# Three edits to an attention, expert and swish kernel: y's sums as a pipeline, a branch with four idle products, a split table moved by one step

## The chip, the cores and the metric

The kernel runs on one core of a Trainium2 chip. The metric is the device time of one execution in microseconds (us), the median over runs; lower is better. An engine has its own instruction queue and works through it in order: PE (TensorE, matrix products), ACT (ScalarE), DVE (VectorE), POOL (GpSimd) and SP (SyncE, which issues most of the DMAs). Engines wait for each other and for DMAs on semaphores.

## The reference, cut to what matters

Attention without softmax over four batches, a top-1 mixture of experts with a fixed number of slots, and a swish layer:

```python
attn = np.maximum(z @ z.T / S, 0) ** 2            # per batch, S = 3072, z is S x 64
x = (u * (attn @ v)).reshape(B * S, 256)
e = argmax(x @ w_gate)                            # 8 experts, 384 slots each
slot[e] <- the first 384 tokens that chose e      # the others give zero rows
y = relu(slot @ w1[e]) @ w2[e] * gate             # 256 -> 1024 -> 256
h = y @ w_in; out = (h * sigmoid(h)) @ w_out      # 256 -> 2048 -> 256
```

All products are fp32: an operand is kept as a high part (rounded to fp32r) and a low part (what is left), and a product is the sum of three products of parts. "To split" a tile is a cast for the high part and a subtraction for the low part.

## The kernel before

**Attention.** The tokens come in chunks: six of 512 (batch 0), then one of 384 (chunk 6, the first of batch 1). A step (`attend`) handles one block of 128 keys: `scores` (two products into a PSUM bank `ps_s`), relu and square on ACT and DVE, `square` (ACT casts `ah`, DVE subtracts `al`) and, three steps after the scores, `values` (six products into `ps_a`). A chunk has KT = 24 steps, so chunk 6 starts at step TL = 144. PE's order within a step is scores, then values.

**The table around the steps.** `at(t, f)` notes work for the end of step t; each engine then gets it in the order in which it was noted. For batch 1, v and z have to be loaded and split again in six groups g of four key blocks: `load_z`, `load_v` (SP), and four steps later `split_z` (POOL) and `split_v` (cast on ACT, subtraction on POOL). The tiles `zr` of `load_z` and `zq` of a chunk's own queries (`Chunk.load`, split by POOL into `qt`) share two buffers; `rawt` for v has two buffers as well (g % 2). A load whose buffer is not yet free makes SP wait, and all loads behind it. POOL also sums up converted weights (`Convert`, L215, L218, L220) and scatters finished token rows (L463).

**The branch.** Expert 0 is computed ahead of the branch (`inward(0, ...)`): its second half `expert_out(d)` ends with a copy of y on ACT (L634) and a store to `yT` by SP (L635), for d = 0 and 1. Then `unless_full` (L949) branches on all engines if a slot is still free; here it never is. Behind the branch stand the transposes of unit 1 (`transposes`, L598) and its hidden products (`hidden`).

**The swish layer.** y is read back by blocks of 1024 slots (`Slots.load`), and seven block products stand in for eight (`quad`): they need sums of y's four blocks, each split in two parts. `Slots.steps` is a generator: b11 and b21 as they are, t1 = b12 - b11, t2 = b22 - t1, t3 = b22 - b12, t4 = b21 - t2, and b22. Before, every `put` casts on ACT (L724) and subtracts on DVE (L725) and every difference (L733, L738, L743, L748) stands in a step of its own, in the order in which the values depend on each other. For the first slots the steps run beside the last unit's `expert_out(0)`, two at a time (`prepare`), and the rest in the first `quad`; later slots take one step for each `side()` of a quad. A `quad` begins with two blocks on b11 and b21, copies the first (`p1`, L1093) on ACT, and goes on with blocks on t2 and t1 into the same bank.

Of the kernel before, what the change touches and what calls it, by code (L numbers as in the profile page):

```python
# [8 lines left out]
F32 = mybir.dt.float32  # L9
# [11 lines left out]
P = 128  # L21


def raw(ap):
    return ap.bitcast(F32)
# [3 lines left out]
def attention_moe_swish_kernel(  # L29
# [13 lines left out]
    nc = tc.nc  # L43
    w_in, w_out = w_in.bitcast(I32), w_out.bitcast(I32)
    B, S, D = v.shape
    E, _, F = w1.shape
    F2 = w_out.shape[0]
    KT = S // P
    GK = 4
    NG = KT // GK  # L50
    NH = D // P
    LAG = 3
    SQ = 4
    QC = 512
    QB = 384
    NTM = QC // P
    FT, FT2 = F // P, F2 // P
    SLOT = -(-cap // P) * P
    NSLOT = E * SLOT
    QM = min(QB, SLOT)  # L60
# [10 lines left out]
    wts = ctx.enter_context(tc.tile_pool(name="wts", bufs=1))  # L71
    dram = ctx.enter_context(tc.tile_pool(name="dram", bufs=1, space=DRAM))
    disp = dram.tile([NSLOT, ROW], F32, name="disp")
    yT = dram.tile([NH, P, NSLOT], F32, name="yT")
# [12 lines left out]
    def bank(kind):  # L87
        return pools["ps_" + kind].tile([P, 512], F32, tag=kind, name="ps_" + kind)
# [63 lines left out]
    wih = wts.tile([P, NH, F2], F32R, name="wih")  # L152
    wil = wts.tile([P, NH, F2], F32R, name="wil")
    wo = wts.tile([P, FT2, 2 * D], F32R, name="wo")

    def head(eng, hi, x):

# [90 lines left out]
    class Stream:  # L248
# [5 lines left out]
        def at(self, t, f):  # L254
            self.todo.setdefault(t, []).append(f)
# [318 lines left out]
    class Unit:  # L574
# [45 lines left out]
        def expert_out(self, d, fs=range(FT)):  # L620

            Q, x = self.Q, self.x
            t = bank("s")
            ds = slice(d * P, (d + 1) * P)
            for n, f in enumerate(fs):
                q, r = divmod(f, FT // 2)
                wh, wl = x.w2h[q][:, r, ds], x.w2l[q][:, r, ds]
                mm(t[:, :Q], lhsT=wh, rhs=hh[f][:, :Q], start=(n == 0), stop=False)
                mm(t[:, :Q], lhsT=wl, rhs=hh[f][:, :Q], start=False, stop=False)
                mm(t[:, :Q], lhsT=wh, rhs=hl[f][:, :Q], start=False, stop=(n == FT - 1))  # L630
                if n % 2:
                    yield
            y = pools["el"].tile([P, QC], F32, tag="r", name="y", bufs=3)
            nc.scalar.copy(y[:, :Q], t[:, :Q])  # L634
            nc.sync.dma_start(out=yT[d][:, self.off:self.off + Q], in_=y[:, :Q])  # L635

# [64 lines left out]
    class Slots:  # L703
# [12 lines left out]
                self.b[d, h] = t  # L716

        def steps(self):
            V = nc.vector
            parts = list(self.parts)  # L720

            def put(n, x):
                hi, lo = self.t[n] = parts.pop(0), parts.pop(0)
                nc.scalar.copy(hi, x)  # L724
                V.tensor_sub(lo, x, raw(hi))  # L725

            b = self.b
            put("b11", b[0, 0])
            yield
            put("b21", b[1, 0])  # L730
            yield
            t1 = self.temps()
            V.tensor_sub(t1, b[0, 1], b[0, 0])  # L733
            yield
            put("t1", t1)
            yield
            t2 = self.temps()
            V.tensor_sub(t2, b[1, 1], t1)  # L738
            yield
            put("t2", t2)  # L740
            yield
            t3 = self.temps()
            V.tensor_sub(t3, b[1, 1], b[0, 1])  # L743
            yield
            put("t3", t3)
            yield
            t4 = self.temps()
            V.tensor_sub(t4, b[1, 0], t2)  # L748
            yield
            put("t4", t4)  # L750
            yield
            put("b22", b[1, 1])
            yield

        def product(self, f, g, j, last):
# [34 lines left out]
    TL = nb0 * KT  # L790
# [11 lines left out]
    def idle(n):  # L802

        nc.tensor.matmul(wps[:, :n], lhsT=warm[:, :P], rhs=warm[:, :n], start=True, stop=True)
# [26 lines left out]
            at(c * KT - (11 if c < nb0 else 8), chunks[c].load)  # L831
            at(c * KT - 6, lambda c=c: chunks[c].split(nc.gpsimd))
    for g in range(NG):

        t = TL - KT + (g + 1) * GK + LAG + 1
        at(t - 4, lambda g=g: (b1.load_z(g), b1.load_v(g)))
        at(t, lambda g=g: (b1.split_z(g, nc.gpsimd, nc.gpsimd), b1.split_v(g, eng=nc.scalar)))

    free = [t for t in range(CV_A, TL + CV_B) if (t < KT or CV_OFF <= (t - LAG + 1) % KT < KT - 1)]
# [84 lines left out]
    if early:  # L924
        inward(0, first, False)
    st.finish()


    def unless_full(label=None):
# [53 lines left out]
    for h in range(NH):  # L983
        u.transposes(h)
        drain()
        u.split_x(h)

    blocks = Blocks()

# [19 lines left out]
    for i in range(first, len(units)):  # L1009
        if i + 1 < len(units):  # L1010

            inward(i, lambda f: next(work, None) if f > 4 and f != FT else None)
        else:
            for _ in work:
                pass
            stage += halves([pools["ut"].tile([P, 1024], F32, tag="ut", name="stage0"),
                             pools["xr"].tile([P, NTM * ROW], F32, tag="xr", name="stage1")])
            slots[0].load()
            n = [0]

            def prepare(f):
                n[0] += 1
                if n[0] == FT:

                    raws = [wts.tile([P, GK * D], F32R, tag=f"rawt{k}", name=f"part{k}") for k in range(4)]
                    sets[0] = halves(raws) + halves(big[0:3])
                    slots[0].parts = sets[0]
                    prepare.it = slots[0].steps()
                if n[0] > FT:
                    for _ in range(2):  # L1030
                        next(prepare.it, None)

            inward(i, prepare)


            second = units[i].expert_out(1, [2, 3, 0, 1] + list(range(4, FT)))
# [201 lines left out]
```

## Time and profile before

| what | value |
|---|---|
| runs before | median 737.92 us of 3 (736.95 to 738.42) |
| the profiled execution's own time | 734.02 us |
| its span | 732.2 us |
| PE busy | 714.6 us (98%) |
| DVE, ACT, POOL busy | 521.4 (71%), 502.8 (69%), 265.9 us (36%) |
| waits of PE that end by another engine | ACT L358: 4.9 us in 2; SP L949: 2.0 us |

Stretches below are in us from the start of the span. In a timeline row the brackets at the end hold the idle time of the engine just before the instruction and what ended it. `x6` stands for six instructions that follow each other. PEclk is the clock that TensorE was granted, as a share of 2.4 GHz; 0.50 is 1.2 GHz. A PE row's length runs to a modelled end; the next product can start before it.

### The profile page before, as it was taken

Reading aid. Unit: us, or ns where it says so; the run is one execution under the profiler, and the core shown is the slowest. Engines: PE = TensorE matmul, PEld = TensorE weight load, DVE = VectorE, ACT = ScalarE, POOL = GpSimd, SP = SyncE. Lnnn points to the kernel's source line nnn. Section 1 sums busy time; section 2 is a strip of 40 time slices with the busy share of each in tenths; the row PEclk is TensorE's granted clock in tenths of the full one; section 3 lists DMA queues with packets and bytes.
Section 4 is the critical chain, followed back from the end, with each engine's and each line's share of the span. In section 5 each row is a group of like instructions: output and inputs, shape, how many; then the busy total and the mean of one; then the engine's idle time right before and its main releaser. Section 6 shows DMA issues by size and latency. Waiting matters only on the chain.

```text
span 732.2 us, 11355 instructions
## 1 busy us (share of the span) xinstructions
PE 714.6 (98%) x3951; PEld 637.7 (87%) x3951; DVE 521.4 (71%) x955; ACT 502.8 (69%) x986; POOL 265.9 (36%) x246
## 2 busy tenths in 40 slices
PE   8999999999999998998999999899999999999996
PEld 6888888888888877998999999799999999999896
DVE  6787877878778765862677777668767876666790
ACT  6777778777787867864666666566557665665671
POOL 7771505314253289254577676000004000040004
PEclk9999999999999999999999999999999999999999
DMA  5833515134155323452555554020101000010001
GB/s 182 288 140 122 181 49 190 51 123 138 41 203 174 116 74 97 133 166 88 206 178 176 178 177 149 12 69 15 44 1 51 9 1 0 1 58 1 1 1 58
DMA packets 50668, 72.18 MB, mean 99 GB/s; under 512 B 3446, under 2 KB 38684, under 8 KB 50608
## 3 DMA queue, kind: packets, MB, share of 16 engines
q1 hardware_dynamic: 48160, 65.03, 27.2%
q0 software_dynamic: 2448, 6.39, 2.4%
q8 instruction: 32, 0.52, 0.3%
q14 instruction: 28, 0.23, 0.1%
HBM read 46.05 MB, written 25.77 MB: 98 GB/s over the span
## 4 chain that ended last, share of the span: by engine, by line
PE 50%; issue 1%; ACT 0%; DVE 0%; POOL 0%; POOLq 0%; DVEq 0%; ACTq 0%
PE ps_s L766 18%; PE ps_a L240 8%; PE ps_s L240 7%; PE ps_a L1050 5%; PE ps_a L1051 5%; PE ps_a L1052 5%; PE ps_a L598 1%; POOL out L777 0%; ACT part L724 0%; POOLq L1234 0%; DVE part L725 0%; DVE temp L743 0%; DVE temp L738 0%; DVE temp L733 0%; ACT u L1093 0%
## 5 line engine op out<-in xcount | busy, mean ns | idle before, releaser
L240 PE MATMUL ps_a<-ah,big 128*128 128x512 f32 (+1 forms) x672 | 184.0, 390 | 4.9 <-ACT ah L358 4.9
L240 PEld LDWEIGHTS ps_a<-ah,big 128*128 128x128 f32 x672 | 124.5, 189 | 26.4 <-ACT ah L358 4.9
L359 DVE TENSOR_TENSOR al<-ps_s,ah 128x512 fp32r<-128x512 f32 (+1 forms) x168 | 111.4, 663 | 29.3 <-ACT ah L358 29.3
L345 ACT ACTIVATE r<-ps_s 128x512 f32<-128x512 f32 (+1 forms) x168 | 98.3, 585 | 44.7 <-PE ps_s L240 39.6
L350 DVE TENSOR_TENSOR ps_s<-ps_s,r 128x512 f32<-128x512 f32 (+1 forms) x132 | 89.2, 676 | 42.8 <-ACT r L345 41.2
L777 POOL DMA_INDIRECT out<-rows,ids x24 | 25.4, 1060 | 244.2 <-ACT rows L774 238.4
L766 PEld LDWEIGHTS ps_s<-wo,big 128*128 128x128 f32 x792 | 103.2, 190 | 5.0
L566 POOL TENSOR_TENSOR big<-rawt,big 128x512 fp32r<-128x512 f32 x64 | 90.3, 1437 | 43.5 <-ACT big L161 42.9
L240 PE MATMUL ps_s<-qt,kz 128*128 128x512 f32 (+1 forms) x336 | 105.6, 391 | 0.0
L766 PE MATMUL ps_s<-wo,big 128*128 128x256 f32 x792 | 105.2, 282 | 0.0
L240 PE MATMUL ps_a<-al,big 128*128 128x512 f32 (+1 forms) x336 | 101.6, 383 | 0.0
L358 ACT CAST ah<-ps_s 128x512 fp32r<-128x512 f32 (+1 forms) x168 | 95.7, 569 | 3.5 <-DVE ps_s L350 3.3
L240 PEld LDWEIGHTS ps_s<-qt,kz 128*128 128x128 f32 x336 | 63.4, 190 | 11.5 <-POOL kz L295 0.4
L240 PEld LDWEIGHTS ps_a<-al,big 128*128 128x128 f32 x336 | 63.1, 189 | 11.6
L463 POOL DMA_INDIRECT disp<-xr,idx x27 | 28.4, 1052 | 107.9 <-ACT ps_s L348 79.8
L240 PE MATMUL ps_a<-qt,big 128*128 128x384 f32 x336 | 61.2, 341 | 0.2 <-ACT qt L604 0.2
L240 PEld LDWEIGHTS ps_a<-qt,big 128*128 128x128 f32 x336 | 59.7, 192 | 0.8 <-ACT qt L604 0.5
L161 ACT CAST big<-rawt 128x512 fp32r<-128x512 f32 x86 | 51.5, 624 | 6.4 <-DMA rawt<-in_v 6.4
L1063 DVE TENSOR_TENSOR sg<-ps_a,sg 128x512 f32<-128x512 f32 x72 | 47.9, 684 | 2.2
L1073 DVE TENSOR_TENSOR big<-sg,big 128x512 fp32r<-128x512 f32 x66 | 45.1, 686 | 6.2 <-ACT big L1072 5.0
L766 PEld LDWEIGHTS ps_s<-wo,late_c 128*128 128x128 f32 x348 | 45.9, 189 | 2.6
L1072 ACT CAST big<-sg 128x512 fp32r<-128x512 f32 x66 | 41.0, 622 | 9.2 <-DVE sg L1063 8.8
(227 smaller groups left out, 1245.5 us busy)
## 6 DMA issues: line engine op xcount, KB each, us to landing
rawt<-in_w SPq DMA_DIRECT2D x32, 512.0 KB, 5.0
out<-zero SPq DMA_DIRECT2D x16, 768.0 KB, 7.3
rawt<-in_v SPq DMA_DIRECT2D x11, 512.0 KB, 4.1
rawt<-in_w_in SPq DMA_DIRECT2D x8, 512.0 KB, 5.1
disp<-empty SPq DMA_DIRECT2D x6, 528.0 KB, 7.1
xg<-disp SPq DMA_DIRECT2D x8, 396.0 KB, 3.3
zr<-in_zT SPq DMA_DIRECT2D x12, 256.0 KB, 4.1
ut<-in_uT SPq DMA_DIRECT2D x6, 512.0 KB, 4.4
```

What stands on the lines that cost most here:

```text
L161: eng.copy(hi, x)
L240: nc.tensor.matmul(*a, **k)
L345: nc.scalar.activation(r[:, :Q], s[:, :Q], AF.Relu)
L350: nc.vector.tensor_mul(s[:, :Q], s[:, :Q], r[:, :Q])
L358: nc.scalar.copy(ah[:, :Q], a[:, :Q])
L359: nc.vector.tensor_sub(al[:, :Q], a[:, :Q], raw(ah[:, :Q]))
L566: nc.gpsimd.tensor_sub(ls[q][:, cs], rawt[r0 + q][:, cs], raw(hs[q][:, cs])))
L766: nc.tensor.matmul(o, lhsT=w[:, cs], rhs=wo[:, f, c:c + D], start=m not in self.seen, stop=last and n == 2, skip_group_check=True)
L1050: nc.tensor.matmul(ps, lhsT=ah, rhs=th, start=start, stop=False, skip_group_check=True)
L1063: nc.vector.tensor_mul(sg, src, sg)
L1072: nc.scalar.copy(gh, g)
L1073: nc.vector.tensor_sub(gl, g, raw(gh))
```

## The change

Three places are edited.

1. `Slots.steps` is written as a pipeline: the low part of a value stands beside the next difference and the next cast. It now has 9 steps, not 11, and `prepare` takes 2, 1, 1, 2 of them at its four calls, not 2 each; with that the cast of t3 and the difference t4 are still the last work ahead of the first quad.
2. The store of expert 0's second y tile (d = 1) is no longer issued ahead of the branch: y stays in a tile of its own (`y0`), and SP gets the store behind the branch's transposes in the program. Four idle products of 512 columns (bf16, `warm`) are put on PE ahead of the branch.
3. The table of batch 1: every load and split of z and v comes one step earlier, but for the split of group 1, which stays where it was.

```diff
--- before.py
+++ after.py
@@ -152,6 +152,8 @@
     wih = wts.tile([P, NH, F2], F32R, name="wih")
     wil = wts.tile([P, NH, F2], F32R, name="wil")
     wo = wts.tile([P, FT2, 2 * D], F32R, name="wo")
+    y0 = wts.tile([P, QM], F32, name="y0")
+    later = []
 
     def head(eng, hi, x):
 
@@ -630,9 +632,14 @@
                 mm(t[:, :Q], lhsT=wh, rhs=hl[f][:, :Q], start=False, stop=(n == FT - 1))
                 if n % 2:
                     yield
-            y = pools["el"].tile([P, QC], F32, tag="r", name="y", bufs=3)
+            keep = self.first and d == NH - 1
+            y = y0 if keep else pools["el"].tile([P, QC], F32, tag="r", name="y", bufs=3)
             nc.scalar.copy(y[:, :Q], t[:, :Q])
-            nc.sync.dma_start(out=yT[d][:, self.off:self.off + Q], in_=y[:, :Q])
+            store = lambda: nc.sync.dma_start(out=yT[d][:, self.off:self.off + Q], in_=y[:, :Q])
+            if keep:
+                later.append(store)
+            else:
+                store()
 
 
 
@@ -716,40 +723,49 @@
                 self.b[d, h] = t
 
         def steps(self):
+
             V = nc.vector
             parts = list(self.parts)
-
-            def put(n, x):
-                hi, lo = self.t[n] = parts.pop(0), parts.pop(0)
-                nc.scalar.copy(hi, x)
-                V.tensor_sub(lo, x, raw(hi))
-
             b = self.b
-            put("b11", b[0, 0])
-            yield
-            put("b21", b[1, 0])
-            yield
-            t1 = self.temps()
-            V.tensor_sub(t1, b[0, 1], b[0, 0])
-            yield
-            put("t1", t1)
-            yield
-            t2 = self.temps()
-            V.tensor_sub(t2, b[1, 1], t1)
-            yield
-            put("t2", t2)
-            yield
-            t3 = self.temps()
-            V.tensor_sub(t3, b[1, 1], b[0, 1])
-            yield
-            put("t3", t3)
-            yield
-            t4 = self.temps()
-            V.tensor_sub(t4, b[1, 0], t2)
-            yield
-            put("t4", t4)
-            yield
-            put("b22", b[1, 1])
+
+            def hi(n, x):
+                self.t[n] = parts.pop(0), parts.pop(0)
+                nc.scalar.copy(self.t[n][0], x)
+
+            def lo(n, x):
+                V.tensor_sub(self.t[n][1], x, raw(self.t[n][0]))
+
+            def diff(x, y):
+                t = self.temps()
+                V.tensor_sub(t, x, y)
+                return t
+
+            hi("b11", b[0, 0])
+            yield
+            lo("b11", b[0, 0])
+            hi("b21", b[1, 0])
+            yield
+            lo("b21", b[1, 0])
+            t1 = diff(b[0, 1], b[0, 0])
+            yield
+            t2 = diff(b[1, 1], t1)
+            hi("t1", t1)
+            yield
+            lo("t1", t1)
+            t3 = diff(b[1, 1], b[0, 1])
+            hi("t2", t2)
+            yield
+            lo("t2", t2)
+            t4 = diff(b[1, 0], t2)
+            hi("t3", t3)
+            yield
+            lo("t3", t3)
+            hi("t4", t4)
+            yield
+            lo("t4", t4)
+            hi("b22", b[1, 1])
+            yield
+            lo("b22", b[1, 1])
             yield
 
         def product(self, f, g, j, last):
@@ -831,9 +847,9 @@
             at(c * KT - (11 if c < nb0 else 8), chunks[c].load)
             at(c * KT - 6, lambda c=c: chunks[c].split(nc.gpsimd))
     for g in range(NG):
-
-        t = TL - KT + (g + 1) * GK + LAG + 1
+        t = TL - KT + (g + 1) * GK + LAG
         at(t - 4, lambda g=g: (b1.load_z(g), b1.load_v(g)))
+        t += g == 1
         at(t, lambda g=g: (b1.split_z(g, nc.gpsimd, nc.gpsimd), b1.split_v(g, eng=nc.scalar)))
 
     free = [t for t in range(CV_A, TL + CV_B) if (t < KT or CV_OFF <= (t - LAG + 1) % KT < KT - 1)]
@@ -924,6 +940,9 @@
     if early:
         inward(0, first, False)
     st.finish()
+    wps = bank("a")
+    for _ in range(4):
+        idle(QC)
 
 
     def unless_full(label=None):
@@ -984,6 +1003,8 @@
         u.transposes(h)
         drain()
         u.split_x(h)
+    for store in later:
+        store()
 
     blocks = Blocks()
 
@@ -1027,7 +1048,7 @@
                     slots[0].parts = sets[0]
                     prepare.it = slots[0].steps()
                 if n[0] > FT:
-                    for _ in range(2):
+                    for _ in range(2 if n[0] in (FT + 1, FT + 4) else 1):
                         next(prepare.it, None)
 
             inward(i, prepare)
```

**DVE, where the sums of the first slots begin** (`part` and `big` are the parts, `stage` the blocks of y, `temp` the differences). Before:

```order
L725 TENSOR_TENSOR part_7299<-stage_7213,part_7299 128x512
L725 TENSOR_TENSOR part_7300<-stage_7213,part_7300 128x512
L733 TENSOR_TENSOR temp<-stage_7214,stage_7213 128x512
L725 TENSOR_TENSOR part_7301<-temp,part_7301 128x512
L738 TENSOR_TENSOR temp<-stage_7214,temp 128x512
L725 TENSOR_TENSOR part_7302<-temp,part_7302 128x512
L743 TENSOR_TENSOR temp<-stage_7214 128x512
L725 TENSOR_TENSOR big_107<-temp,big_107 128x512
L1094 TENSOR_TENSOR ps_a<-ps_a,u_7347 128x512
```

Now, on the same engine:

```order
L736 TENSOR_TENSOR part_7304<-stage_7218,part_7304 128x512
L736 TENSOR_TENSOR part_7305<-stage_7218,part_7305 128x512
L740 TENSOR_TENSOR temp<-stage_7219,stage_7218 128x512
L740 TENSOR_TENSOR temp<-stage_7219,temp 128x512
L736 TENSOR_TENSOR part_7306<-temp,part_7306 128x512
L740 TENSOR_TENSOR temp<-stage_7219 128x512
L736 TENSOR_TENSOR part_7307<-temp,part_7307 128x512
L740 TENSOR_TENSOR temp<-stage_7218,temp 128x512
L1115 TENSOR_TENSOR ps_a<-ps_a,u_7353 128x512
```

The second difference (t2) moved ahead of the first low part, t3 ahead of the low part of t2, and t4 ahead of the first quad's addition (L1094, now L1115).

**SP, the loads for batch 1 from group 2's v on** (`zq` is chunk 6's, `zr` group 3, 4, 5, `rawt0` and `rawt1` take v in turn). Before:

```order
L287 DMA rawt0_129<-in_v 128x4x256
L143 DMA out_0<-zero_105 768x1x256
L327 DMA zq_3034<-in_zT 128x384
L281 DMA zr_3042<-in_zT 128x512
L287 DMA rawt1_130<-in_v 128x4x256
L281 DMA zr_3123<-in_zT 128x512
L287 DMA rawt0_129<-in_v 128x4x256
```

Now:

```order
L289 DMA rawt0_129<-in_v 128x4x256
L143 DMA out_0<-zero_105 768x1x256
L283 DMA zr_3024<-in_zT 128x512
L289 DMA rawt1_130<-in_v 128x4x256
L329 DMA zq_3044<-in_zT 128x384
L283 DMA zr_3107<-in_zT 128x512
L289 DMA rawt0_129<-in_v 128x4x256
```

Group 3's z and v moved ahead of chunk 6's `zq`; so group 3's z takes the buffer that group 1's split sets free, `zq` the one of group 2's split, and group 4's z the one of `zq`'s split.

**ACT, around the cast of group 4** (`big8`), with relu (`r`) and `ah` of the steps 143 to 145. Before:

```order
L345 ACTIVATE r_3161<-ps_s_3158 128x512
L348 ACTIVATE ps_s_3158<-r_3161 128x512
L358 CAST ah_3164<-ps_s_3142 128x512
L345 ACTIVATE r_3177<-ps_s_3174 128x384
L358 CAST ah_3180<-ps_s_3158 128x512
L161 CAST big8_115<-rawt0_129 128x512 x2
```

Now:

```order
L347 ACTIVATE r_3161<-ps_s_3158 128x512
L350 ACTIVATE ps_s_3158<-r_3161 128x512
L360 CAST ah_3164<-ps_s_3142 128x512
L163 CAST big8_115<-rawt0_129 128x512 x2
L347 ACTIVATE r_3178<-ps_s_3175 128x384
L360 CAST ah_3181<-ps_s_3158 128x512
```

The cast moved ahead of the relu of step 144 and of the `ah` of step 143.

## Rows read from the trace of the kernel before

**Rows 1.** Windows: stretch, us, busy PE, PEld, DVE, ACT, POOL, PEclk, DMA share, GB/s.
```profile
273.74:278.06 4.32, 0.00 (x2) 0.00 (x1) 0.50 (x1) 2.16 (x5) 4.16 (x6) 1.00 0.63 200
279.05:282.46 3.41, 3.41 (x10) 2.81 (x10) 2.78 (x5) 3.16 (x7) 3.25 (x4) 0.50 0.11 26
...
340.44:342.49 2.05, 0.01 (x1) 0.03 (x1) 0.00 (x0) 0.48 (x1) 0.19 (x1) 1.00 0.27 98
343.90:347.31 3.41, 3.41 (x12) 3.14 (x11) 1.24 (x3) 2.49 (x5) 0.24 (x1) 0.50 0.52 132
...
464.76:466.81 2.05, 0.00 (x0) 0.00 (x1) 1.19 (x3) 1.48 (x3) 0.00 (x0) 0.99 0.00 0
466.80:470.20 3.40, 3.39 (x9) 2.84 (x10) 2.54 (x4) 2.22 (x4) 0.00 (x0) 0.50 0.15 58
```

**Rows 2.** Timeline at the first slots: start, us, engine, line, operation, [idle before, what ended it].
```profile
461.25 0.62 ACT L724 CAST part<-temp 128x512 fp32r<-128x512 f32 x1 [1.50 <-DVE temp L733]
...
461.91 0.69 DVE L725 TENSOR_TENSOR part<-temp,part 128x512 fp32r<-128x512 f32 x1 [0.74 <-ACT part L724]
...
465.27 0.62 ACT L724 CAST big<-temp 128x512 fp32r<-128x512 f32 x1 [1.36 <-DVE temp L743]
...
466.17 0.59 ACT L1093 COPY u<-ps_a 128x512 f32<-128x512 f32 x1
...
466.81 0.80 PE L1050 MATMUL ps_a<-part,comb_ah 128*128 128x512 f32 x1 [2.05 <-ACT u L1093]
```

**Rows 3.** Waits of SP's queue around the branch: who, for whom, us, times, longest.
```profile
SPq L635 <- ACTq L949: 3.1, 1, 3.1
```

**Rows 4.** Line L949, the branch: sequencer events, ns, first and last start.
```profile
L949 PEldq EVENT_SEMAPHORE  x2: 51/51/51, 340.5 to 340.6; - x2
...
L949 PEldq COMPARE_BRANCH  x1: 383/383/383, 337.2 to 337.2; - x1
```

**Rows 5.** Timeline behind the branch, PE.
```profile
342.49 0.85 PE L598 MATMUL ps_a<-ident,xg 128*128 128x128 f32 x6 [2.04 <-SPq L949]
```

**Rows 6.** Groups by form, first 8 us: idle products, granted 1.2 GHz there; busy, mean ns.
```profile
L804 PE MATMUL ps_s<-warm 128*128 128x512 bf16 x7 | 3.2, 630 | 1.3 <-DVE warm L794 1.3
```

**Rows 7.** Timeline around steps 138 to 144, by engine: POOL and SP.
```profile
261.91 2.74 POOL L301 TENSOR_TENSOR big<-rawt,big 128x512 fp32r<-128x512 f32 x2
...
270.02 1.30 POOL L295 TENSOR_TENSOR kz<-zr,kz 64x512 fp32r<-64x512 f32 x1
...
274.49 0.99 POOL L335 TENSOR_TENSOR qt<-zq,qt 128x384 fp32r<-128x384 f32 x1
...
271.34 0.34 SPq L281 DMA_DIRECT2D zr<-in_zT  x1
...
275.94 0.38 SPq L287 DMA_DIRECT2D rawt<-in_v  x1
```

**Rows 8.** The same stretch: ACT and PE.
```profile
267.99 0.58 ACT L358 CAST ah<-ps_s 128x512 fp32r<-128x512 f32 x1
...
275.90 1.14 ACT L161 CAST big<-rawt 128x512 fp32r<-128x512 f32 x2 [6.36 <-DMA rawt<-in_v]
...
271.31 0.62 PE L240 MATMUL ps_s<-qt,kz 128*128 128x512 f32 x2
...
273.13 0.61 PE L240 MATMUL ps_s<-qt,kz 128*128 128x512 f32 x2
278.06 1.25 PE L240 MATMUL ps_a<-ah,big 128*128 128x512 f32 x4 [4.32 <-ACT ah L358]
```

**Rows 9.** DMA issues, 225 to 300 us: KB each, median us from issue to landing.
```profile
rawt<-in_v SPq DMA_DIRECT2D x4, 512.0 KB, 4.0
...
zq<-in_zT SPq DMA_DIRECT2D x1, 192.0 KB, 2.5
```

**Rows 10.** Waits, whole span: who, for whom, us in total, times, longest.
```profile
ACT u L1093 <- PE ps_a L1052: 28.2, 20, 1.6
...
DVE ps_a L1094 <- PE ps_a L1052: 16.2, 19, 1.1
```

## The prediction

> **What bounds the kernel now.** PE is busy for 98% of the span, so a change to another engine pays only where PE stands still or runs at its lower clock. I read the windows first, around every idle stretch of PE over 2 us; there are three [rows 1]. In each the busy PE column is zero, and within some 1.5 us behind each follows a stretch of 3.4 us whose granted clock is 0.50, that is 1.2 GHz, while PE is busy all through it. Such a stretch does half of its work, so it costs 3.41 / 2 = 1.7 us on top of the idle time. Then I read the timeline at each of the three places for what ended the idle time: ACT's copy p1 at the first slots [rows 2], SP at the branch [rows 5], and at the end of batch 0 ACT's `ah`, which stood on ACT behind a cast that waited 6.36 us for a load of v [rows 8]. Each edit touches one of these places, so the sum has three terms.
>
> **Term 1, y's sums.** The last rows of the chain before are: cast of t1 at 461.25, cast of t3 at 465.27, y's copy and p1's copy at 466.17, PE at 466.81 [rows 2]. From t1's cast to t3's are 4.02 us for two sums, 2.01 each: a cast (0.62), a low part (0.69) and the next difference (as long), each waiting for the one before; the brackets show ACT idle for 1.4 to 1.5 us, then DVE for 0.74 us. Now DVE already has t2 when ACT is done with t1, and t3's difference follows the low part of t1: from t1's cast on 0.62 + 0.69 + 0.69 = 2.0 us to t3's cast. It moves from 465.27 to about 463.3, and p1's copy with it, to 464.2 with its end at 464.8. PE has other products until 464.76, so about 0.1 us of the 2.05 us is left. Gain 1.95 us; never more than 2.05, and 1.4 if each sum saves only one low part. The low clock behind it should go as well, since nothing else idles there: 1.7 us. What the new order puts into the way is t4's cast (0.62 us) ahead of the sigmoid and of the second copy (u2). u2's copy then ends at about 464.8 + 0.6 + 0.6 + 0.6 = 466.6. PE needs it after six products of 512 columns and six of 384; with 1.82 us for a step of eight products of 512 [rows 8] those take 1.37 + 1.02 = 2.4 us, until 467.2. It hides, with 0.6 us to spare. Later slots take the same subtractions and casts in fewer steps; I cost that at nothing, because DVE and ACT wait for PE at the head of a quad [rows 10], and price its failure below. Term 1: -3.65 us (bounds -1.4 and -3.75).
>
> **Term 2, the branch.** SP waits 3.1 us for the second y tile before it can store it and branch [rows 3], and PE's first transposes wait for SP [rows 5]: behind the branch SP settles the DMA semaphores, one by one, that these transposes check. PE had taken its own branch at 337.2 and was through its own two checks at 340.6 [rows 4]. With the store behind the branch SP is 3.1 us earlier and off the path. Nothing reads this tile before the swish layer's `Slots.load`. The queue behind the store moves with PE. What is late next is PE itself. Four idle products: seven of them took 3.2 us at 1.2 GHz [rows 6], 0.46 each, so 0.23 at 2.4 GHz and 0.9 for four, to 341.35. The two checks come 0.05 and 0.2 us after the last product as before, and some 0.2 us are left for the checks ahead of the transposes: they start at 341.75 in place of 342.49. Gain 0.7 us. The idle products cost 0.9 us of path and buy PE work in a stretch that had none; without them the checks could come up to 0.9 us earlier. With 0.4 us idle in place of 2.05 I take the low clock as gone: 1.7 us. Term 2: -2.4 us (bounds -2.85, with the transposes right behind the idle products, and +0.9, below).
>
> The Trainium skill (Runtime: NRT & Kernel Launch, section on instruction fetch mechanics) says that a taken branch whose target has not been fetched stalls until its page has come. By that rule the idle time would be the fetch, and moving SP's store would not shorten it. The rows speak against it here: PE's branch was taken over 3 us before its last product ended [rows 4].
>
> **Term 3, the table of batch 1.** Here POOL sets the pace. Before, group 3's z waited for the split of group 2, which ended at 270.02 + 1.30 = 271.32: SP issued it at 271.34, v behind it [rows 7], and ACT's cast started at 275.90 [rows 8]. Now that z takes the buffer of group 1's split, which is over before 261.91, and v waits only for POOL's subtractions of group 1, until 261.91 + 2.74 = 264.65 [rows 7]. A load of v takes 4.0 us [rows 9], so it lands at 268.65, and ACT comes to the cast, one step earlier, at 267.99 + 0.58 = 268.57. This wait goes. But `zq` now waits for the split of group 2 (271.32), lands 2.5 us later [rows 9] at 273.8, just when POOL is done with group 2's subtractions (some 2.6 us from 271.35), so its split ends at 275.48 as before [rows 7], and group 4's z and v, behind it on SP, are issued when they were: v at 275.94 [rows 7], landing at 279.94. Two things get late:
> - Chunk 6's first scores. A step takes 273.13 - 271.31 = 1.82 us [rows 8]; without the stall they are due at 273.13 + 1.82 = 274.95, their second product at 275.1, and it needs the low part of `zq`: 0.4 us idle.
> - The cast of group 4, now at step 143. ACT is there at 273.74 + 3 x 0.59 = 275.5 (relu, square and `ah` behind the scores at 273.13) and waits until 279.94, with all that is queued behind it on ACT. Before, PE went on 2.16 us after such a cast had started (275.90 to 278.06) [rows 8]: now at 282.1. PE's own work lasts from 275.5 over two groups of values (1.37 each) and three of scores (0.34 for a pair of 384, half of it for the first) to 279.1. Idle 3.0 us.
>
> Idle before: the values were due at 273.13 + 0.46 = 273.59 and came at 278.06, 4.5 us. Now 3.4 us in two pieces. Gain 1.1 us; the second piece is longer than the two late stalls of 2.05 us, so I leave the lower clock behind it as it was. Bounds: +0.4 if `zq` needs the 4.0 us of a v load, since POOL, `zq`'s split and v shift by 1.5 us; -2.8 if the clock holds. Term 3: -1.1 us.
>
> **Sum.** -3.65 - 2.4 - 1.1 = -7.15 us. Against the profiled execution's own 734.02 us that is 726.9. The median of the runs is 3.9 us above this execution, and no row says where those lie, so I take the difference from the median: 737.92 - 7.15 = **730.8 us**, 1% faster. A measurement of this kernel tells about 0.2%, 1.5 us, from no change.
>
> **The rivals.**
> - *The late clock stays low (0.14).* One of the two late stretches is granted 1.2 GHz although its idle time is gone; the transposes and the casts behind the branch leave PE thin. 730.8 + 1.7 = 732.5. Against it: each such stretch in rows 1 has at least 2 us of idle time ahead of it.
> - *The branch is paid in full (0.10).* PE stands 2.05 us behind the idle products as it did behind the last real one, whatever SP does; the transposes start at 343.4, 0.9 us late, and the clock falls as before. Term 2 is +0.9: 734.1. For it: no row shows PE's way past the branch alone. Against it: rows 4. The instruction-fetch rule of the Trainium skill, named above, would give this case.
> - *The stall in batch 1 goes altogether (0.07).* Group 4's v is there in time, for a free buffer. Term 3 is then -4.5 - 1.7: 725.7. Against it: `zq`'s split ends at 275.48 and the cast is due at 275.5; a load takes 4.0 us.
> - *The quads begin to wait; slower (0.04).* A step of the later slots' sums now often puts two subtractions at a time in front of a quad's own DVE work. If each of the 18 steps (nine for each of two slots) held PE by one subtraction, 0.69 us, that is 12.4 us: 743.2. It decides from 11 waiting steps on. For it: PE has no idle time to give there. Against it: DVE stands 16.2 us in 19 waits for PE at a quad's head, 0.85 each, and ACT 1.4 us [rows 10], more than a subtraction.
> - *Nothing measurable (0.05).* The sums are late again for another link, such as y's copy, and the branch is paid: 736.4 to 739.4.
>
> **How the numbers follow.** The forecast, with the clock of term 3 either way and its loads a little early or late, has 0.60 and lies at 728.5 to 732.5. Faster: 0.60 + 0.14 + 0.10 + 0.07 = 0.91. Same 0.05, slower 0.04. The range from 727.8 to 734.4 leaves out the full gain in batch 1, the slower rival and no change, 0.16 together.
>
> **What would show it.** Right: p1's copy ends within 0.2 us of PE's other products, and no stretch at 0.50 behind it; SP's store of y0 stands behind the branch and PE's transposes start 0.4 us after the idle products; the cast of group 3 does not wait, that of group 4 waits over 4 us for v, and PE's longest idle time is some 3 us at a place three steps later. Wrong: an idle PE of over 1 us at the branch or at the first slots; the cast of group 4 without a wait; idle time between the quads, or a wait of POOL for `zq`.

## The result, and the profile after

The changed kernel takes 730.47 us (median of 6 runs, 727.94 to 730.67); the kernel before took 737.43 us beside it (6 runs, 733.70 to 738.42). The ratio is 0.9904 with an interval of 0.9876 to 0.9931: faster by 1.0%, 7.0 us, where 7.15 us and 730.8 us were forecast. The profiled execution of the changed kernel took 727.94 us, with a span of 726.2 us.

The windows of the changed kernel at the places of [rows 1] come first (stretch, us, busy PE, PEld, DVE, ACT, POOL, PEclk, DMA share, GB/s). The one idle stretch of 4.32 us in batch 1 is now two, of 0.51 and 2.55 us; at the branch 0.56 us are left behind the dummies; at the first slots nothing is left. In the stretches of 3.41 us behind each, where 0.50 stood, the granted clock is 1.00.

```profile
275.14:275.65 0.51, 0.00 (x1) 0.00 (x1) 0.17 (x1) 0.31 (x1) 0.51 (x2) 1.00 0.00 0
279.53:282.08 2.55, 0.00 (x1) 0.00 (x0) 0.49 (x2) 2.05 (x5) 2.47 (x3) 1.00 0.33 96
282.08:285.49 3.41, 3.41 (x17) 2.89 (x18) 3.41 (x8) 2.86 (x7) 3.33 (x4) 1.00 0.39 130
339.16:339.72 0.56, 0.00 (x1) 0.03 (x1) 0.00 (x0) 0.00 (x0) 0.19 (x1) 1.00 0.11 31
340.80:344.21 3.41, 3.41 (x18) 3.11 (x19) 1.79 (x4) 3.38 (x7) 0.55 (x1) 1.00 0.68 209
458.51:460.56 2.05, 2.04 (x12) 1.54 (x10) 1.70 (x4) 1.54 (x4) 0.00 (x0) 1.00 0.00 0
460.56:463.97 3.41, 3.41 (x16) 3.02 (x17) 3.11 (x5) 2.58 (x5) 0.00 (x0) 1.00 0.15 58
```

To see where time came from, follow one product through both traces: its start after, less its start before. The difference grows where time is gained.

| a product at (before) | after minus before, us | what lies between it and the row above |
|---|---|---|
| 260.21, chunk 5 | -0.14 | |
| 330.03, expert 0 | -2.17 | batch 1's table |
| 342.49, first transposes | -2.77 | idle time at the branch |
| 350.07, first unit | -4.22 | the 1.2 GHz stretch behind it |
| 466.81, first slots | -6.25 | idle time at the first slots |
| 470.53 | -7.77 | the 1.2 GHz stretch behind it |
| 640.02 | -7.56 | |
| 724.05, last products | -5.99 | two late pieces, 0.5 and 1.1 us lost |

The first slots, timeline: the row that answers to the casts and the copy in [rows 2].

```profile
457.04 1.34 ACT L733 CAST part<-temp 128x512 fp32r<-128x512 f32 x2 [1.50 <-DVE temp L740]
...
459.02 0.62 ACT L733 CAST big<-temp 128x512 fp32r<-128x512 f32 x1 [0.63 <-DVE temp L740]
...
459.92 0.59 ACT L1114 COPY u<-ps_a 128x512 f32<-128x512 f32 x1
...
460.56 0.50 PE L1071 MATMUL ps_a<-part,comb_ah 128*128 128x512 f32 x1
```

The first row merges the casts of t1 and t2, and the cast of t3 comes 1.98 us behind the start of t1's, as forecast (2.0; it was 4.02). p1's copy ends at 460.51, while PE is still in its other products, and PE goes on without a gap.

The branch, timeline, against [rows 3, 5]: the store now stands behind the branch, and it is no longer SP that PE waits for: the profile names PE's own checks (PEq).

```profile
338.12 1.04 PE L820 MATMUL ps_a<-warm 128*128 128x512 bf16 x3
...
338.82 0.35 SPq L638 DMA_DIRECT2D yT<-y  x1
...
339.72 0.84 PE L600 MATMUL ps_a<-ident,xg 128*128 128x128 f32 x6 [0.56 <-PEq L968]
```

Batch 1, timeline by engine, against [rows 7, 8].

```profile
274.59 1.00 POOL L337 TENSOR_TENSOR qt<-zq,qt 128x384 fp32r<-128x384 f32 x1
...
275.62 0.34 SPq L283 DMA_DIRECT2D zr<-in_zT  x1
276.06 0.38 SPq L289 DMA_DIRECT2D rawt<-in_v  x1
...
268.46 1.15 ACT L163 CAST big<-rawt 128x512 fp32r<-128x512 f32 x2
...
280.03 1.14 ACT L163 CAST big<-rawt 128x512 fp32r<-128x512 f32 x2 [4.58 <-DMA rawt<-in_v]
...
275.65 0.44 PE L242 MATMUL ps_s<-qt,kz 128*128 128x384 f32 x1 [0.51 <-POOL qt L337]
...
282.08 1.19 PE L242 MATMUL ps_a<-ah,big 128*128 128x512 f32 x4 [2.55 <-ACT ah L360]
```

Group 3's cast (268.46) waits for nothing, group 4's waits 4.58 us for its v, which SP issued behind group 4's z, and z waited for the split of `zq` (274.59 + 1.00). PE resumes at 282.08; 282.1 was forecast.

Against this stand losses near the end, which no step of the forecast has. The larger is 0.85 us of idle time: the first of two copies of output rows on ScalarE comes 1.1 us later than its place in the trace before, after 3.61 us for which the profile names PE, whose products had ended 0.4 us earlier. The timeline there:

```profile
715.50 0.65 ACT L790 COPY rows<-ps_s 128x256 f32<-128x256 f32 x2 [3.61 <-PE ps_s L782]
715.92 2.57 PEld L782 LDWEIGHTS ps_s<-wo,big 128*128 128x128 f32 x21 [1.05 <-ACT rows L790]
715.92 2.78 PE L782 MATMUL ps_s<-wo,big 128*128 128x256 f32 x21 [0.85 <-ACT rows L790]
```

### The profile page after: what moved, and what is told of

Its sections match the earlier page's. It is cut to its first block, busy times and chain, and to the rows that moved or that the text cites. A ratio compares the mean times of both kernels' runs of the same rounds, so it can differ in the third digit from the quotient of the medians.

```text
span 726.2 us, 11358 instructions
## 1 busy us (share of the span) xinstructions
PE 712.7 (98%) x3954; PEld 634.3 (87%) x3955; DVE 521.0 (72%) x955; ACT 502.6 (69%) x986; POOL 264.7 (36%) x246
## 4 chain that ended last, share of the span: by engine, by line
PE 51%; issue 1%; POOL 0%; POOLq 0%; ACT 0%
PE ps_s L782 18%; PE ps_s L242 8%; PE ps_a L242 8%; PE ps_a L1071 6%; PE ps_a L1072 5%; PE ps_a L1073 5%; PE ps_a L600 1%; POOL out L793 0%; POOLq L1255 0%; ACT qt L606 0%; POOLq L793 0%
## 5 line engine op out<-in xcount | busy, mean ns | idle before, releaser
L1094 DVE TENSOR_TENSOR big<-sg,big 128x512 fp32r<-128x512 f32 x66 | 45.1, 687 | 7.1 <-ACT big L1093 5.8
```

The source lines that it names most:

```text
L1094: nc.vector.tensor_sub(gl, g, raw(gh))
```

## The experiments

The theory is that of the forecast: three separate waits, one edit for each, and behind each wait a stretch at 1.2 GHz that goes with it. The rivals: the parts work only together; the dummies, not the store, free the branch; the clock falls whatever the idle time is. The four parts were first put, each alone, on the kernel before.

**The sums alone.** The edit is `Slots.steps` and the counts of `prepare`, as in the diff of the change.

> Part one alone on the kernel before: the sums of y's blocks as a pipeline, with the step counts that go with it. Theory: 3.6 us faster than the kernel before (2.0 us of idle TensorE ahead of the first swish products, and 1.7 us of the 3.41 us stretch at 1.2 GHz behind it, which goes too); TensorE idle at that place under 0.2 us, the other two idle stretches and their two low-clock stretches as before. Rival, the clock falls there whatever the idle time: 2.0 us faster. Rival, the three parts only work together: nothing measurable (under 1.5 us).

Measured: 734.58 us (7 runs, 732.71 to 734.94), ratio 0.9953 (0.9937 to 0.9969), 3.5 us by the ratio. At the first slots PE has no idle time and no stretch at 0.50 follows (windows below); the other two idle stretches, 4.13 and 1.93 us, kept theirs. The theory holds, and this part does not need the others.

```profile
463.31:465.36 2.05, 2.04 (x11) 1.55 (x9) 1.70 (x4) 1.53 (x4) 0.00 (x0) 1.00 0.00 0
465.36:468.77 3.41, 3.41 (x16) 3.02 (x17) 3.11 (x5) 2.59 (x5) 0.00 (x0) 1.00 0.15 58
```

**The store alone.**

```diff
-            y = pools["el"].tile([P, QC], F32, tag="r", name="y", bufs=3)
+            keep = self.first and d == NH - 1
+            y = y0 if keep else pools["el"].tile([P, QC], F32, tag="r", name="y", bufs=3)
...
+    for store in later:
+        store()
```

> The store of the first unit's last y tile moved behind the branch, without the dummy products. Theory: the branch waited for SyncE's wait for that tile alone, so the transposes start about 1.5 us earlier after the last product (idle 0.5 us in place of 2.05) and the low clock behind it goes: 3.2 us faster than before, and the dummies of the full change cost more path than they return. Rival, the dummies are what covers TensorE's own way past the branch: TensorE still stands some 2 us and the time is that of the kernel before (within 0.5 us). Rival, the idle time goes but the clock falls all the same: 1.5 us faster.

Measured: 733.13 us (12 runs, 732.29 to 737.26), ratio 0.9951 (0.9935 to 0.9966), 3.6 us. PE's last product ends at 340.27, and on the timeline the transposes follow 0.61 us behind:

```profile
340.81 0.35 SPq L638 DMA_DIRECT2D yT<-y  x1
...
340.88 0.88 PE L600 MATMUL ps_a<-ident,xg 128*128 128x128 f32 x6 [0.61 <-ACTq L956]
```

The windows of this version (the branch, then the first slots) show that the clock holds behind the branch without any dummy:

```profile
340.27:340.88 0.61, 0.00 (x0) 0.00 (x1) 0.00 (x0) 0.48 (x1) 0.00 (x0) 1.00 0.00 0
342.00:345.41 3.41, 3.41 (x18) 3.12 (x19) 1.80 (x4) 3.38 (x7) 0.55 (x1) 1.00 0.65 191
462.03:464.07 2.04, 0.00 (x1) 0.00 (x0) 1.18 (x3) 1.48 (x3) 0.00 (x0) 1.00 0.00 0
464.24:467.65 3.41, 3.41 (x17) 3.02 (x18) 3.03 (x5) 2.23 (x5) 0.00 (x0) 1.00 0.15 58
```

So the store is what the branch waited for. What is left ends by ScalarE (ACTq): its copy of y fills 0.48 of the 0.61 us, and its checks at the branch follow at 340.8 and 340.9. By the rule on instruction fetch of the Trainium skill (Runtime: NRT & Kernel Launch, section on instruction fetch mechanics), as the prediction used it, the 2.04 us of [rows 5] would still stand here; the trace does not agree, 0.61 us are left. That speaks against this reading, not against the rule: PE takes its branch here (it jumps over the block for slots that are still free), the program marks it as likely taken, and PE took it over 3 us before its last product ended [rows 4]. The last two rows hold a surprise: 2.04 us idle at the first slots, with nothing edited there, and the clock stayed at 1.00 behind them.

**The dummies alone.**

```diff
     st.finish()
+    wps = bank("a")
+    for _ in range(4):
+        idle(QC)
```

> The four dummy products alone, with the store where it was. Theory: SyncE's wait for the y tile still sets the start of the transposes, so the dummies lie beside it: TensorE idle 1.1 us in place of 2.05 at the branch, transposes not earlier; the time is that of the kernel before, or 1.7 us less if an idle stretch of 1.1 us no longer brings the 1.2 GHz stretch. Rival, the branch is paid behind the dummies in full: idle 2 us again and 0.9 us slower.

Measured: 736.25 us (12 runs, 734.20 to 738.74), ratio 0.9993 (0.9976 to 1.0009): no difference that can be told. The transposes start at 342.31, where they did (342.49), behind 1.05 us of idle time; SP still ends the wait. The timeline's row and the windows behind the branch and at the slots:

```profile
342.31 0.85 PE L598 MATMUL ps_a<-ident,xg 128*128 128x128 f32 x6 [1.05 <-SPq L952]
```

```profile
343.39:346.80 3.41, 3.41 (x18) 3.12 (x19) 1.79 (x4) 3.38 (x7) 0.55 (x1) 1.00 0.44 112
464.00:466.05 2.05, 0.00 (x0) 0.00 (x1) 1.19 (x3) 1.49 (x3) 0.00 (x0) 1.00 0.00 0
466.22:469.63 3.41, 3.41 (x10) 2.84 (x11) 2.68 (x5) 2.22 (x4) 0.00 (x0) 0.50 0.15 58
```

Here the price of a low stretch can be read twice, between executions that wait alike. At the branch the transposes start 0.18 us earlier than before and the product at 350.07 starts 1.62 us earlier: 1.44 us for the stretch at 0.50 that is gone (0.9 us of it is given back near 366, where PE idles 0.58 us in this execution, and late pieces near 653 and 724 take the rest, so what the clock gives back does not show in this execution's time). At the first slots this version and the one with the store alone both idle for 2.04 and 2.05 us, and only this one falls to 0.50: their distance grows from 1.98 us to 3.52 us, 1.54 us. The forecast took 1.7.

**The table of batch 1 alone.** The edit is the `t` of the loop over groups, as in the diff of the change.

> The table of batch 1 alone: groups of v one step earlier but for group 1. By the prediction: 1.1 us faster, with idle pieces of 0.4 and 3.0 us in place of 4.3 us and the 1.2 GHz stretch behind left. By the changed kernel's trace (pieces of 0.51 and 2.55 us, no low clock in that execution): 1.2 us faster where the clock falls and 2.9 where it does not, so runs of two kinds, some 1.7 us or a little more apart. Rival: the loads of batch 1 come out late in some other place and nothing is gained.

Measured: 735.26 us (12 runs, 733.52 to 736.72), ratio 0.9971 (0.9959 to 0.9982), 2.1 us. PE's products for expert 0, at 330.03 before, start 2.17 us earlier. Idle pieces of 0.37 and 2.32 us, and behind the second the clock holds:

```profile
281.91:285.32 3.41, 3.41 (x17) 2.89 (x18) 3.41 (x8) 2.88 (x7) 3.33 (x4) 1.00 0.40 121
341.96:345.37 3.41, 3.41 (x11) 3.41 (x12) 0.90 (x2) 2.17 (x4) 0.61 (x1) 0.50 0.54 150
```

The four ratios add up to 1.32%, 9.7 us, against 7.0 of all together. Their intervals, some 2 us either way on both sides, do not tell the two apart. Two things in the traces would make the sum too large: the store-alone execution also kept its clock at the first slots, which the sums count again (1.5), and the dummies cost 0.9 of path where the store no longer waits (next).

**Without the dummies.** The full change less the three lines above.

> The full change without the four dummy products. Theory (from the store alone, where the transposes came 0.61 us after the last product): the dummies add 0.9 us of path and shorten no wait, so the transposes start 0.9 us earlier against the last real product and the kernel is 0.9 us faster than the changed kernel, some 7.8 us faster than the kernel before. Rival: the dummies hold the clock up; without them the 1.2 GHz stretch comes back behind the branch and it is 0.8 us slower than the changed kernel.

Measured: 729.15 us (6 runs, 728.67 to 730.16), ratio 0.9889 (0.9873 to 0.9906). Its interval overlaps that of the full change, so the time alone does not tell them apart; the trace does. The transposes follow the last real product by 0.64 us, and the product that starts at 342.36 in the full change starts at 341.48 here, 0.9 us earlier, with 0.1 us of that from ahead of the branch. The clock stays at 1.00. In this execution 0.6 us is given back near 362, in an idle piece of 0.32 us that the versions below, which have no dummies either, do not show. The branch, timeline:

```profile
338.81 0.86 PE L600 MATMUL ps_a<-ident,xg 128*128 128x128 f32 x6 [0.64 <-ACTq L965]
```

**v ahead of z in batch 1.**

```diff
-        at(t - 4, lambda g=g: (b1.load_z(g), b1.load_v(g)))
+        at(t - 4, lambda g=g: (b1.load_v(g), b1.load_z(g)))
```

> The full change, and in batch 1 SyncE issues the load of v ahead of that of z. Theory: group 4's v stood on SyncE behind its z, which waited for the split of zq (275.62); its own buffer was free at 273.88, so it is issued 2.2 us earlier, lands near 277.9, TensorE resumes near 279.9 and of the idle 2.55 us some 0.4 are left: 2.1 us faster than the changed kernel, and up to 1.7 more in the runs in which the clock fell there. Rival: the z of group 3 or the load of zq, now behind a v, comes late and takes it back: TensorE idle at a z or a zq by 1 us or more, no gain.

Measured: 728.47 us (5 runs, 727.81 to 729.72), ratio 0.9879 (0.9860 to 0.9898). Group 4's v is issued at 273.75 and of the 2.55 us only 0.37 are left, as expected, but the wait came back one group later (timeline, SP, ACT and PE):

```profile
273.75 0.38 SPq L289 DMA_DIRECT2D rawt<-in_v  x1
...
282.52 0.38 SPq L289 DMA_DIRECT2D rawt<-in_v  x1
...
286.38 1.14 ACT L163 CAST big<-rawt 128x512 fp32r<-128x512 f32 x2 [3.14 <-DMA rawt<-in_v]
...
288.61 0.50 PE L392 MATMUL ps_a<-identw,ut 128*128 128x136 f32 x2 [1.54 <-ACT xr L398]
```

Group 5's v waits for the buffer that GpSimd frees with its subtractions of group 3 (until 282.50), so ScalarE's cast stands, with the copies of `xr` behind it. By the products for expert 0 PE is only 0.2 us ahead of the changed kernel. The expectation is missed: the wait moved.

**Both edits.** The full change without the dummies and with v ahead of z.

> The full change without the dummy products and with v issued ahead of z in batch 1. Theory: the two gains add up, 3.0 us or more faster than the changed kernel, near 727 us. Rival: what is gained ahead of the branch is taken back by the next wait there, and only one of the two shows.

Measured: 728.43 us (5 runs, 727.39 to 729.60), ratio 0.9874 (0.9854 to 0.9893). 0.56 us idle at group 4 and 1.37 us at 287.7; in the trace the gain is the dummies' (from the branch on 0.8 us), and the rival is nearer than the theory.

**Copies added on ScalarE.** In the traces of the four versions with one part each and of the changed kernel, late idle pieces of PE stand in front of the same few copies of ScalarE, up to 1.37 us near 650 and 0.9 us near 720; the trace of [rows 1] has none. Without the dummies one of them stands ahead of another copy, at 560 us.

```diff
+    pad = wts.tile([1, 2], F32, name="pad")
...
+    nc.vector.memset(pad, 0.0)
+    for t in range(30, 78):
+        at(t, lambda: nc.scalar.copy(pad[:, 1:2], pad[:, 0:1]))
```

> The full change with 48 copies of one element more on ScalarE in the first four chunks. It asks what the idle pieces are that stand near 644 to 652 us and near 715 to 724 us in five profiled executions of six, in front of the same instructions of ScalarE (numbers 898, 903 and 983 of its 986). If they belong to a place in ScalarE's instruction stream (its code being brought in), they move with the count, to instructions some 48 earlier in the program. If they belong to that point of the work (another engine's or a store's traffic), they stay ahead of the same copies. The time is that of the changed kernel, or up to 2 us more if the copies delay ScalarE's casts in the chunks.

Measured: 735.35 us (10 runs, 733.34 to 737.75), ratio 0.9975 (0.9958 to 0.9991): the 48 copies cost 4.1 us by 200 us and 6 by 300 us, more than expected. The pieces stay in front of the same copies (numbers 946, 951 and 1031 of 1034, 48 later than in the other versions). The timelines of ScalarE with the store alone and with the copies:

```profile
648.87 0.58 ACT L1120 COPY u<-ps_a 128x512 f32<-128x512 f32 x1 [1.23 <-remote]
```

```profile
651.79 0.58 ACT L1136 COPY u<-ps_a 128x512 f32<-128x512 f32 x1 [1.25 <-remote]
```

They stay at a point of the work and do not go with a count in ScalarE's stream. "remote" means that the profile found no releaser.

**Both kernels again.** The last four versions are the changed kernel and the kernel before, unaltered, and two meant to be faster. They ran on another chip (number 14) than the eight versions above (number 3).

> The changed kernel once more, unaltered, on the same chip as the versions of this call. It asks which of its two kinds of runs (728 and 730.5 us) is the usual one and what lies between them. Theory: its pace is set by the idle pieces in front of ScalarE's copies near 560, 645 and 715 us (1.35, 1.35 and 0.85 us), so a profiled execution near 730.5 us shows one 1.35 us piece more than the one near 728. Rival: the clock falls behind the 2.5 us stall in the slower kind, and the profile shows a 3.41 us stretch at 1.2 GHz near 282 us.

> The kernel before once more, unaltered, for a profile. Theory: its profiled execution (734.02 us, 3.4 us under its median) was one without the idle pieces that nine other executions show in front of ScalarE's copies; a usual one, near 737 us, shows 1.3 us near 652 us and 0.85 us near 724 us. Rival: these pieces come with the edits, and the kernel before has none of them.

Measured: the changed kernel 726.37 us (6 runs, 726.20 to 726.90), ratio 0.9907 (0.9886 to 0.9927); the kernel before 733.80 us (11 runs, 731.68 to 735.28), its profiled execution 731.78. Both kernels are about 4 us faster here than above (737.5 and 737.3 for the kernel before on the first chip), and none of the four profiled executions here has a late piece. The window of the changed kernel over the place where 1.35 us stood elsewhere is full:

```profile
643.00:652.00 9.00, 9.00 (x63) 8.34 (x62) 5.62 (x9) 5.08 (x10) 1.25 (x2) 1.00 0.08 29
```

So the pieces do not come from the edits alone: all eight versions on the first chip have some, whichever part of the change they hold, and none of the four here has one, with the change or without. That the chip or its surroundings make them is an argument, not shown. A rival is left: neither of the two profiled executions of the kernel before has a piece, and the only one whose chip is known ran on the second, so the edits could bring them on the first. What they are stays open. Neither of the two expectations was met in its theory: the changed kernel's six runs lie within 0.7 us, and its rival, a fall of the clock behind the 2.4 us stall, did not show either.

The windows of the kernel before in this second execution (branch, then first slots, the idle stretch and the 3.41 us behind it):

```profile
340.34:342.27 1.93, 0.00 (x1) 0.03 (x1) 0.00 (x0) 0.48 (x1) 0.14 (x1) 1.00 0.25 98
342.85:346.26 3.41, 3.30 (x12) 2.84 (x11) 1.02 (x2) 2.89 (x6) 0.00 (x0) 0.50 0.17 18
464.16:466.21 2.05, 0.00 (x1) 0.00 (x0) 1.19 (x3) 1.49 (x3) 0.00 (x0) 1.00 0.00 0
466.21:469.62 3.41, 3.41 (x16) 3.02 (x17) 3.03 (x5) 2.11 (x4) 0.00 (x0) 1.00 0.15 58
```

Between these two executions, free of late pieces, the product differences are -2.0 us for batch 1, -0.5 and -0.8 at the branch (idle time; and clock, 1.1 less 0.3 given back near 366) and -2.0 at the first slots, 5.3 us together. Nothing is gained from the clock at the slots, because the kernel before did not lose it there this time.

**VectorE takes a share of GpSimd's low parts.** Both versions have no dummies and v ahead of z; the subtractions of group 3's v, or of groups 2 and 3, go to VectorE.

```diff
-        def split_v(self, g, n=512, eng=nc.gpsimd, c0=0, c1=GK * D):
+        def split_v(self, g, n=512, eng=nc.gpsimd, c0=0, c1=GK * D, eng2=nc.gpsimd):
...
-                nc.gpsimd.tensor_sub(big[2 * g + 1][:, cs], rawt[g % NR][:, cs], raw(big[2 * g][:, cs]))
+                eng2.tensor_sub(big[2 * g + 1][:, cs], rawt[g % NR][:, cs], raw(big[2 * g][:, cs]))
...
-        at(t, lambda g=g: (b1.split_z(g, nc.gpsimd, nc.gpsimd), b1.split_v(g, eng=nc.scalar)))
+        at(t, lambda g=g: (b1.split_z(g, nc.gpsimd, nc.gpsimd), b1.split_v(g, eng=nc.scalar, eng2=nc.vector if g in (2, 3) else nc.gpsimd)))
```

> No dummy products, v ahead of z in batch 1, and VectorE instead of GpSimd takes the low part of group 3's v. Theory: with v ahead of z the wait moved to group 5's v, whose buffer GpSimd freed only at 282.5 by its subtractions for group 3; on VectorE these follow ScalarE's casts near 270, so v of group 5 is issued some 6 us earlier, the 1.5 us idle piece near 287 goes, and of the stall in batch 1 only 0.5 and 0.4 us are left: 3 us faster than the changed kernel, near 727 us. Rival: 1.4 us more on VectorE in chunk 5 delays its low parts of the scores there, and TensorE waits for them by as much.

> As the version before, with group 2's low part on VectorE too. Theory: group 4's v is then issued right behind the load of zq, at 271.5, and its cast does not wait at all; the 0.4 us piece near 280 goes as well and it is 0.4 us faster than with group 3 alone. Rival: VectorE's 1.4 us more near 262, where it has little idle time, delay the scores there by as much as is gained: the same time or slower.

Measured beside the changed kernel's 726.20 to 726.90: with group 3 on VectorE 725.14 us (5 runs, 724.50 to 726.01), ratio 0.9891 (0.9868 to 0.9914); with groups 2 and 3, 724.28 us (5 runs, 723.82 to 725.83), ratio 0.9884 (0.9860 to 0.9908). Every run of both lies below every run of the changed kernel, by 1.2 and 2.1 us in the medians, though the two intervals against the kernel before overlap with its own. In the traces 1.0 and 0.8 us come from batch 1 (by 300 us), of the 2.4 us of stall that were to be had, and 0.8 us in each from the branch without dummies. With group 3 alone 3 us were expected: the piece near 287 is gone, but 0.50, 0.64 and 0.28 us are idle ahead of it. With both groups the stall at group 4 is gone altogether, and the rival holds as well: PE now waits for VectorE, earlier. The timeline of that version, PE, DVE and POOL:

```profile
266.93 0.73 PE L242 MATMUL ps_a<-al,big 128*128 128x512 f32 x2 [1.46 <-DVE al L361]
...
269.85 0.73 PE L242 MATMUL ps_a<-al,big 128*128 128x512 f32 x2 [0.82 <-DVE al L361]
...
261.86 2.38 DVE L303 TENSOR_TENSOR big<-rawt,big 128x512 fp32r<-128x512 f32 x2
...
272.51 1.28 DVE L303 TENSOR_TENSOR big<-rawt,big 128x512 fp32r<-128x512 f32 x2
...
262.00 3.39 POOL L303 TENSOR_TENSOR big<-rawt,big 128x512 fp32r<-128x512 f32 x2
```

The same two subtractions take VectorE 1.28 us at 272.51 and 2.38 us at 261.86, where GpSimd runs its own of the same shape (3.39 us, 2.50 to 2.74 elsewhere); at 272.51 GpSimd is idle. The Trainium skill (SBUF — State Buffer, section on SBUF's two separate sides) says that a VectorE operation with two SBUF inputs and a GpSimd operation that reads SBUF share a pair of ports, which one of them holds for a whole instruction. The trace agrees in direction, not in full: together the two pairs end 3.53 us after the first began, while one behind the other they would take 1.28 + 2.55 = 3.83 us.

## Why the prediction was right, step by step

**Term 1, -3.65 us.** Idle time: 1.95 us forecast, 2.03 measured. t3's cast came 1.98 us behind t1's, and t4's cast ahead of the sigmoid delayed nothing. Clock: 1.7 forecast, 1.5 measured in the first pair of traces, nothing in the second, where the kernel before kept its clock. The sums alone gave 3.5 us.

**Term 2, -2.4 us.** Idle time: -0.6 us (second pair -0.5) against -0.7; clock: 1.4 and 1.1 us, the latter 0.8 in the end, against 1.7. The mechanism, SP's wait for the store, is shown by the two halves of the edit. One sentence was wrong: the dummies "buy PE work in a stretch that had none". The clock holds in all five versions that move the store without dummies, the store alone among them; the path they were said to take, 0.9 us, they do take: 0.8 us, in the first version without them and in that with group 3 on VectorE.

**Term 3, -1.1 us.** This is the mis-sized term: 2.0 to 2.2 us measured. Its idle times were near (0.4 and 3.0 forecast, 0.51 and 2.55 measured, so 1.3 us gained instead of 1.1), but the step "I leave the lower clock behind it as it was" failed. The argument was that 3.0 us is longer than the 2.05 us that brought a fall elsewhere. The stall of 2.3 to 2.6 us brought none in the changed kernel (two executions), without dummies, and with the table alone; only the version with added copies fell behind it. The price of the clock was off as well: beside the idle time saved (1.3 to 1.6 us) the clock gave back 0.5 to 0.8 us by difference, not the 1.7 with which the bound of -2.8 counts.

**The sum.** In the first pair of traces PE gained 7.8 us up to 470 us and lost 1.8 behind it, most of it in the late pieces, which the execution of [rows 1] does not have. Taking the difference from the median and not from that execution's own 734.02 us was the right choice: the median of the runs lay 3.9 us above that profile, and for the changed kernel 2.5 us above its own. What the text could not place, "no row says where those lie", is not settled. The late pieces may be a part. The granted clock of the single runs points to another: of the kernel before's eleven runs on the second chip, the five at 0.992 took 731.7 to 732.4 us and the four at 0.989 took 734.4 to 735.3; the changed kernel's two fastest, 727.9 and 728.2 us, had 0.999, its other four, 730.4 to 730.7 us, 0.993 to 0.996.

That 7.0 us lies so near to 7.15 is in part luck: term 3 came out 0.9 us larger than forecast, term 2 some 0.4 smaller, the late losses stood in no term, and the clock of term 1 is gained only where the kernel before loses it.

**The rivals.** The late clock did not stay low. The branch was not paid in full: 0.56 us. The stall in batch 1 did not go altogether, for the reason given: its v was late. "Nothing measurable" is ruled out by the interval, and by the trace at the first slots and at the branch. The quads did not wait: from 470.53 to 640.02 PE lost 0.2 us, and nothing in the second pair (-5.54 us at 470 and -5.51 at 640), where 12.4 us stood as the price.

## What to carry to other kernels

Where one engine settles the end of a stage for all, look at what its queue still holds at that point: one store, in the wrong place by a few instructions, held a branch, and idle products laid over the wait did not shorten it. When a load is late because of a buffer, find who frees the buffer and how far that engine lags; putting the load earlier in the queue moves the wait to the next group unless that engine is relieved too. And profile the kernel before a second time, on the chip of the versions beside it, before explaining a difference of some tenths of a per cent: here its first profiled execution lay 3.9 us under its median, and the second came from another chip than most versions.

## What was not expected of the hardware

The length of an idle stretch did not decide by itself whether TensorE was granted 1.2 GHz behind it. Over all profiled executions, idle stretches of 4.1 to 4.3 us brought the lower clock in 5 of 5, those of 2.3 to 2.6 us in 1 of 5, those of 1.9 to 2.1 us in 7 of 9 (4 of 4 at the branch, 3 of 5 at the first slots), and those of 1.0 to 1.6 us in none of 11. With the sums alone it fell during the idle stretch in batch 1 and lasted 6.83 us, in all others of these cases 3.41. Why 2.4 us of idle time was mostly harmless in batch 1 and 2.0 us mostly not at the other two places stays open.

A stretch of 3.41 us at half clock cost 1.44 and 1.54 us where it could be isolated, 1.1 us at the branch in the second pair of traces and 0.5 to 0.8 us, by difference, in batch 1, not the 1.7 that half of its length gives. That PE is not the only limit in such a stretch is an argument, not shown.
